# Two of eight batches turn their probabilities on TensorE instead of through DRAM, under new instruction orders

## The chip, the cores and the metric

The kernel runs on one core of a Trainium2 chip. Five engines of that core work from one program each, in order: PE (TensorE), DVE (VectorE), ACT (ScalarE), POOL (GpSimd) and SP (SyncE, which here only starts DMA transfers). They meet through semaphores. The metric is the time of one execution in microseconds (us). Three runs of the kernel before gave 583.65 us in the median (582.97 to 585.76). One more execution was taken by the hardware profiler, and all rows below come from it.

## The reference

The inputs q, k, v are (8 batches, 8 heads, 576 tokens, 64), in float32. Keys and values are first averaged over groups of 8 tokens, so that each of the 576 queries sees only 72 keys:

```python
k_p = k.reshape(B, H, 72, 8, D).mean(axis=3); v_p = ...the same of v
scores = scale * (q @ k_p.T); attn = softmax(scores); attn_out = attn @ v_p
x = attn_out, heads side by side            # (8, 576, 512)
h = relu(x @ w_in); u, v = halves of h      # w_in 512 x 1024
v_n = (v - mean(v)) / sqrt(var(v) + 1e-6)   # over the 512 features
v_s = w_spatial @ v_n + b_spatial           # 576 x 576, over the tokens
out = (u * v_s) @ w_out                     # w_out 512 x 512
```

w_in and w_out arrive in float64, the rest in float32. The spatial product mixes all tokens of a batch, so it starts only when the whole batch has been normalised.

## The kernel before

**Batches and stages.** Each batch goes through attention (capital letters) and then the gated block (small letters). K and V load and pool keys and values; KT turns the pooled keys; W splits the values; Q0 to Q3 load the queries, one per pair of heads (g); S0 to S3 are the scores and softmax of 512 tokens of such a head pair, U0 and U1 those of the last 64 tokens for two g at once; T0, T1 (512 tokens) and Y0, Y1 (the last 64) turn the probabilities of two g so that keys lie on partitions; A00 to A13 multiply probabilities with values (first digit: half of the tokens, second: g) and leave the result in xT. Then v0 to v4 (the v half of w_in, normalised), u00 to u13, s00 to s13 (the spatial product) and o0 to o4 (w_out). The weights are loaded and split in parts named wv, wu (w_in), wo (w_out), ws (w_spatial) and wb (bias). `warm` (wd) runs matmuls whose result nobody reads.

**Precision.** A product that has to be as good as float32 is made of three faster ones: each operand is split into a rounded high part and a low part (`split`: ACT writes the high part, DVE subtracts it from the source to get the low part), and TensorE adds high x high, low x high and high x low. This is why each stage of attention is followed by work on ACT and DVE.

**What sets the order.** Each stage is a Python generator that hands out a few instructions at each step. Three strings, FIRST, STEP and LAST, say which stage makes its next step; `-` and `+` shift the batch. FIRST runs the lead (loads, all weights, the first batch up to its first outputs), STEP runs once for each of six batches, and LAST ends the program. The instructions of each engine run in just that order. The marks `~^!%` behind a name choose another way of doing a stage: `^` pools on TensorE (`pool_pe`, L304) and loads queries by rows, to be turned on TensorE; any mark on V or K puts the pooling on POOL (`pool_sum`, L293 and L298) unless it is `^`. The mark that counts is the one at the first mention of the stage.

**The turning of probabilities before.** Softmax leaves a tile `e` with tokens on partitions and keys along the free axis; `pt_p` holds the last 8 keys of each head, copied on POOL. The matmul of A wants keys on partitions. In `att_pt` (T) DVE transposes blocks of 32x32 (tile X, L541; XR, L545), a DMA writes the tile to DRAM (xd, L549), and other DMAs read it back with the blocks in their places (pt_l, L556; pt_r, L560). `split_pt` then makes the high parts on ACT (pt_h L525, pt_rr L526) and the low parts on DVE (pt_l L528, pt_rr L531). `att_pt_l` (Y) does the same for the last 64 tokens (XL L569, xdl). The tiles pt_h, pt_l, pt_r and pt_rr have one buffer each, so the second pair of g (T1) can be written only after A has read the first pair (T0). A block layout goes with it: the pooled values lie on partitions in the order (key, block), and `half_of` says for each partition to which head of the pair it belongs.

**Shared buffers.** PSUM has three tiles `mm` (L304, weights, v, u, s, o), three tiles `tp` (transposes, U, A) and one `s` tile for the scores of S. The staging tiles `st` for keys, values, w_out and w_spatial share a ring of three; `g`, which DVE writes after each spatial product (L711), has three; ACT copies it rounded into gT (L717) and POOL writes the rest (gT, L720), which the o stage reads.

## Time and profile before

| what | value |
|---|---|
| median of 3 runs | 583.65 us (582.97 to 585.76) |
| the profiled execution's own time | 583.07 us |
| its span, first to last instruction | 581.3 us |
| so outside the span | 1.8 us |
| first matmul of v0 | 70.19 us |
| end of the last matmul | about 577.7 us |

How to read the rows that follow. The page opens with busy time per engine and then cuts the span into 40 slices of 14.5 us; each digit is a busy share in tenths, and PEclk is the clock that TensorE was granted. A row of grouped instructions reads: line, engine, operation, output tile <- input tiles, shapes, count, then busy us and mean ns of one, then the engine's idle time just before them and what ended it. A row of a timeline starts with the start time and the duration in us. A matmul's duration overlaps with the next one's, so the pace of matmuls is read from their starts. A row of waits gives the total, the number of times and the longest. A row of windows gives, for a stretch of time, its length, then busy time and count for PE, PEld, DVE, ACT and POOL, then the granted clock, the DMA share and GB/s.

### The profile page before, as it was taken

To read this page: it belongs to the slowest core of one execution; us is meant where nothing else is said; L and a number is where in the kernel's file an instruction comes from. 1 tells how busy PE (TensorE), PEld (TensorE's weight loads), DVE (VectorE), ACT (ScalarE), POOL (GpSimd) and SP (SyncE) were. 2 spreads that over 40 slices of the span, in tenths; PEclk is the share of its full clock that TensorE was granted. 3 is DMA by queue.
4 is the path that set the end of the run, shared out by engine and by line. 5 is a ranking of instruction groups with operands and counts; after the bars stand their busy time and mean duration, and the time that the engine had idled before them with its cause. 6 is when DMAs were issued, how large, how long until landed. Compare 5 with 4: busy or idle time off the path is not lost.

```text
span 581.3 us, 10183 instructions
## 1 busy us (share of the span) xinstructions
PE 554.3 (95%) x3428; PEld 499.6 (86%) x3428; DVE 395.5 (68%) x942; ACT 279.1 (48%) x832; POOL 247.2 (43%) x331
## 2 busy tenths in 40 slices
PE   5975899898999999999999999999999999999997
PEld 5865788796899889998899879988899889988995
DVE  2698789986875686868775877588776857433320
ACT  2545668834563355444553546435544475323321
POOL 3336576494655414433453325442643325303340
PEclk9796899999999999999999999999999999999999
DMA  8978624676753346234733356344622140200102
GB/s 228 262 212 230 144 77 117 171 211 173 215 122 89 98 134 132 54 95 164 188 67 95 127 147 124 84 104 150 124 55 74 73 115 24 75 36 1 37 2 90
DMA packets 134372, 68.61 MB, mean 118 GB/s; under 512 B 89136, under 2 KB 114736, under 8 KB 134320
## 3 DMA queue, kind: packets, MB, share of 16 engines
q1 hardware_dynamic: 134320, 67.96, 43.8%
q8 instruction: 27, 0.44, 0.3%
q14 instruction: 25, 0.20, 0.1%
HBM read 47.87 MB, written 20.05 MB: 117 GB/s over the span
## 4 chain that ended last, share of the span: by engine, by line
PE 82%; DVE 5%; DMA 5%; SPq 3%; POOL 2%; issue 1%; ACT 1%; DVEq 0%; ACTq 0%; POOLq 0%
PE mm L687 16%; PE mm L644 16%; PE mm L729 16%; PE mm L706 15%; PE s_ps L494 5%; PE mm L660 3%; DMA qt<-in_q 2%; PE tp L505 2%; PE tp L592 1%; PE mm L304 1%; PE tp L595 1%; PE mm L707 1%; PE mm L708 1%; PE tp L593 1%; PE tp L594 1%
## 5 line engine op out<-in xcount | busy, mean ns | idle before, releaser
L687 PE MATMUL mm<-xT,win_h 128*128 128x256 f32 (+1 forms) x512 | 103.6, 296 | 0.3 <-DVE wT_l L169 0.3
L720 POOL TENSOR_TENSOR gT<-g,gT 128x256 fp32r<-128x256 f32 x64 | 48.8, 765 | 87.7 <-ACT gT L717 87.7
L687 PEld LDWEIGHTS mm<-xT,win_h 128*128 128x128 f32 x512 | 82.8, 188 | 2.3 <-DVE wT_l L169 0.5
L729 PE MATMUL mm<-wout_h,gT 128*128 128x512 f32 x256 | 81.9, 400 | 0.6 <-POOL gT L720 0.6
L644 PE MATMUL mm<-win_h,xT 128*128 128x512 f32 x256 | 81.7, 400 | 0.0
L487 POOL TENSOR_TENSOR e<-e,rs 128x576 f32<-128x576 f32 (+1 forms) x48 | 49.1, 1022 | 71.4 <-DVE rs L485 56.1
L706 PE MATMUL mm<-wT_h,vn_h 128*128 128x256 f32 (+1 forms) x256 | 76.1, 297 | 2.4 <-ACT ru L690 2.4
L706 PE MATMUL mm<-wT_h,vn_l 128*128 128x256 f32 (+1 forms) x256 | 75.4, 295 | 0.0
L706 PE MATMUL mm<-wT_l,vn_h 128*128 128x256 f32 (+1 forms) x256 | 75.3, 294 | 0.0
L687 PE MATMUL mm<-xT,win_l 128*128 128x256 f32 (+1 forms) x256 | 75.3, 294 | 0.0
L711 DVE TENSOR_TENSOR g<-mm,ru 128x256 f32<-128x256 f32 (+1 forms) x64 | 28.6, 451 | 56.0 <-PE mm L708 48.9
L654 POOL TENSOR_TENSOR vn_l<-vv,vn_h 128x512 fp32r<-128x512 f32 x32 | 43.5, 1367 | 39.6 <-ACT vn_h L652 39.5
L717 ACT ACTIVATE gT<-g 128x256 fp32r<-128x256 f32 x64 | 26.3, 415 | 68.9 <-DVE g L711 68.9
L644 PEld LDWEIGHTS mm<-win_h,xT 128*128 128x128 f32 x256 | 46.8, 188 | 11.2 <-issue 1.0
L729 PEld LDWEIGHTS mm<-wout_h,gT 128*128 128x128 f32 x256 | 46.7, 188 | 11.3 <-issue 1.0
L631 POOL TENSOR_TENSOR rstd<-rstd,neg_half 128x1 f32<-128x1 f32 (+1 forms) x40 | 25.3, 635 | 72.2 <-DVE rstd L629 65.2
L706 PEld LDWEIGHTS mm<-wT_h,vn_h 128*128 128x128 f32 x256 | 48.2, 188 | 3.1 <-ACT ru L690 2.6
L644 PE MATMUL mm<-win_l,xT 128*128 128x512 f32 x128 | 50.6, 395 | 0.0
L729 PE MATMUL mm<-wout_l,gT 128*128 128x512 f32 x128 | 50.6, 395 | 0.0
L167 ACT ACTIVATE xT<-tp 128x320 fp32r<-128x320 f32 (+1 forms) x64 | 25.2, 410 | 51.8 <-PE tp L595 50.1
L706 PEld LDWEIGHTS mm<-wT_h,vn_l 128*128 128x128 f32 x256 | 48.2, 188 | 0.2
L687 PEld LDWEIGHTS mm<-xT,win_l 128*128 128x128 f32 x256 | 48.1, 188 | 0.0
(175 smaller groups left out, 1305.2 us busy)
## 6 DMA issues: line engine op xcount, KB each, us to landing
qt<-in_q SPq DMA_DIRECT2D x116, 72.0 KB, 3.1
st<-in_k SPq DMA_DIRECT2D x32, 256.0 KB, 3.1
st<-in_v SPq DMA_DIRECT2D x32, 256.0 KB, 4.7
xd<-X SPq DMA_DIRECT2D x32, 256.0 KB, 2.2
pt_l<-xd SPq DMA_DIRECT2D x32, 256.0 KB, 3.2
out<-ob SPq DMA_DIRECT2D x32, 256.0 KB, 2.1
stw<-in_moe_w_in SPq DMA_DIRECT2D x8, 512.0 KB, 5.9
pt_r<-xdr SPq DMA_DIRECT2D x32, 64.0 KB, 3.3
```

The source lines that it names most:

```text
L167: nc.scalar.activation(hi, src, AF.Copy)
L487: nc.gpsimd.tensor_tensor(em, em, rs.unsqueeze(2).broadcast_to([m, n, SP]), op=ALU.mult)
L494: nc.tensor.matmul(s_ps[:, c // 2, (c % 2) * 2 * SP:(c % 2 + 1) * 2 * SP], lhsT=t["q", g][:, c * P:(c + 1) * P], rhs=kp_bd[:, g, :], start ...
L631: nc.gpsimd.tensor_tensor(rstd[:m], rstd[:m], neg_half[:m], op=ALU.pow)
L644: nc.tensor.matmul(a, lhsT=xT[:, i, o + c * P:o + (c + 1) * P], rhs=w[:, i, DH:], start=(i == 0 and j == 0), stop=(i == NK - 1 and j == 2))
L654: nc.gpsimd.tensor_tensor(t["vn_l"][:, c, :], vv, f32(t["vn_h"][:, c, :]), op=ALU.subtract)
L687: nc.tensor.matmul(a, lhsT=w[:, i, d * P:(d + 1) * P], rhs=xT[:, i, o + ts.start:o + ts.stop], start=(i == 0 and j == 0), stop=(i == NK - ...
L706: nc.tensor.matmul(a, lhsT=x[:, c, ds], rhs=y[:, c, ts], start=(c == 0 and j == 0), stop=False)
L711: nc.vector.tensor_tensor(g, a, t["ru"][:, d, ts], op=ALU.mult)
L717: nc.scalar.activation(dst[:, d, 0, at:at + m], g[:, o:o + m], AF.Copy)
L720: nc.gpsimd.tensor_tensor(dst[:, d, 1, at:at + m], g[:, o:o + m], f32(dst[:, d, 0, at:at + m]), op=ALU.subtract)
L729: nc.tensor.matmul(a, lhsT=src[:, i, x, at:at + m], rhs=w[:, i, :], start=(i == 0 and j == 0), stop=(i == ND - 1 and j == 2))
```

## The change

1. **T and Y of batches 0 and 1** (`b < PE_B`, 2). PE turns the probabilities with the identity: for T, four transposes of 128x128 for each g and four of the last 8 keys (new lines L548, L552), into three `tp` tiles; for Y, two and one (L600, L601). ACT then writes pt_h and pt_rr straight from PSUM and DVE subtracts from PSUM. X, xd, and the reading back are gone for these two batches. Batches 2 to 7 keep the way through DRAM.
2. **The values of these two batches** are loaded in plain row order (one DMA for two g, where there were two), so that keys lie on partitions as the transposes leave them; `half` holds two versions of the head mask.
3. **warm** runs three more matmuls in float32r per call, but its calls fall from five (wd3, wd8, wd14, wd18, wd19, four matmuls of 128x128 in float32 each) to one (wd0).
4. **All three strings are new**, so each engine has another order throughout. The marks change with them: values of batches 2 to 7 are now pooled on POOL in all six batches (before in two), keys of batches 2 to 7 on DVE; one more query tile and one more split of a weight go through TensorE.

Three places in the new orders matter for what follows. The first is PE in the lead, around the scores S3 of batch 0 (L494 before, L501 now). Before:

```order
L304 MATMUL mm<-st,ident 128x128 x8
L505 MATMUL tp<-kp_bd,pt_q 64x144 x2
L266 MATMUL mm<-ident 128x128 x8
L494 MATMUL s_ps<-kp_bd,qT 128x144 x4
L304 MATMUL mm<-st,ident 128x128 x8
L304 MATMUL mm<-st_r,ident 64x64 x8
L592 MATMUL tp<-pt_h,vm_h 128x256
```

and now:

```order
L501 MATMUL s_ps<-kp_bd,qT 128x144 x4
L548 MATMUL tp<-ident,e 128x128 x8
L552 MATMUL tp<-ident,pt_p 32x128 x4
L304 MATMUL mm<-st,ident 128x128 x8
L512 MATMUL tp<-kp_bd,pt_q 64x144 x2
L304 MATMUL mm<-st,ident 128x128 x8
L304 MATMUL mm<-st_r,ident 64x64 x8
L636 MATMUL tp<-pt_h,vm_h 128x320
```

The scores S3 are followed at once by the transposes T0; the key pooling of batch 1 (L304) and U1 (L512) moved behind them, ahead of the first A (L636); the warm matmuls (L266) are gone from here.

The second is SP at the start of the program, the DMAs in the order in which they are started. Before:

```order
L327 DMA st<-in_k 128x1x512 x4
L183 DMA stw<-in_moe_w_in 128x1024
L314 DMA st_r<-in_k 64x1x512
L425 DMA qt<-in_q 128x4x64 x2
L426 DMA qt<-in_q 64x2x64
```

and now:

```order
L181 DMA stw<-in_moe_w_in 128x1024
L327 DMA st<-in_k 128x1x512 x2
L181 DMA stw<-in_moe_w_in 128x1024
L327 DMA st<-in_k 128x1x512 x2
L314 DMA st_r<-in_k 64x1x512
L432 DMA qt<-in_q 128x4x64 x2
L433 DMA qt<-in_q 64x2x64
```

A chunk of w_in (512 KB) now goes ahead of each half of batch 0's keys.

The third is POOL in the body, where batch n's spatial products are followed by the subtraction into gT while batch n+2's values arrive. Before (batch 3, the last whose values were pooled on POOL):

```order
L654 TENSOR_TENSOR vn_l<-vv,vn_h 128x512 x2
L487 TENSOR_TENSOR e<-e,rs 128x576
L498 COPY pt_p<-e 128x64
L720 TENSOR_TENSOR gT<-g,gT 128x256 x2
L720 TENSOR_TENSOR gt<-g,gt 128x64
L293 TENSOR_TENSOR st_r<-st_r 64x256
L293 TENSOR_TENSOR st_r<-st_r 64x128
L298 TENSOR_TENSOR vq<-st_r 64x64
L720 TENSOR_TENSOR gT<-g,gT 128x256 x4
```

and now, from the values of batch 4 on:

```order
L505 COPY pt_p<-e 128x64
L764 TENSOR_TENSOR gT<-g,gT 128x256 x2
L293 TENSOR_TENSOR st<-st 128x2x256
L293 TENSOR_TENSOR st<-st 128x2x128
L298 TENSOR_TENSOR vp<-st 128x128
```

The six instructions of a batch's main values (the last three rows, then the same three for the other two g) now stand between the second and the third gT, for batches 4 to 7; the values of batches 2 and 3 are spread over the lead.

The diff; in the strings only the first line of FIRST is shown, since the numbers in them tell a reader little:

```diff
--- before.py
+++ after.py
@@ -24,54 +24,49 @@
 FIRST = (
-    "-K^ -K wv0~% -K -K -Q1^ wv0 -K wv2~^ -Q1 -K wv2 -K -Q0^ wv0 wv0 -V^ wv1 -V -Q1 -KT~ -KT -Q0 K^ -KT wv0 "
...
+    "wv1~% wv1 -K^ wv1 wv0^% wv1 -K -K wv0 -Q0~^ wu3 wv0 -Q1^ -K -K -Q0 -K -K wd0 -KT~ -Q2^ -Q0 wo0^! -KT -KT "
...
 STEP = (
...
 LAST = (
...
@@ -140,13 +135,16 @@
     nc.gpsimd.memset(f32(vb[TL:]), 1.0)
 
 
-    half_of = const.tile([P, 2], F32, name="half_of")
+
+    half = const.tile([P, 2, 2], F32, name="half")
+    nc.vector.tensor_reduce(half[:, 0, 0:1], ident[:, :SP], axis=AX.X, op=ALU.add)
     by_block = ident.rearrange("p (s k) -> p k s", k=4)
     nb, ns = divmod(SP, 32)
-    nc.vector.tensor_reduce(half_of[:, 0:1], by_block[:, :nb, :], axis=AX.XY, op=ALU.add)
-    nc.vector.tensor_reduce(half_of[:, 1:2], by_block[:, nb, :ns], axis=AX.X, op=ALU.add)
-    nc.vector.tensor_tensor(half_of[:, 0:1], half_of[:, 0:1], half_of[:, 1:2], op=ALU.add)
-    nc.vector.tensor_scalar(half_of[:, 1:2], half_of[:, 0:1], -1.0, 1.0, op0=ALU.mult, op1=ALU.add)
+    nc.vector.tensor_reduce(half[:, 1, 0:1], by_block[:, :nb, :], axis=AX.XY, op=ALU.add)
+    nc.vector.tensor_reduce(half[:, 1, 1:2], by_block[:, nb, :ns], axis=AX.X, op=ALU.add)
+    nc.vector.tensor_tensor(half[:, 1, 0:1], half[:, 1, 0:1], half[:, 1, 1:2], op=ALU.add)
+    nc.vector.tensor_scalar(half[:, :, 1:2], half[:, :, 0:1], -1.0, 1.0, op0=ALU.mult, op1=ALU.add)
+    PE_B = 2
 
     mask = const.tile([2 * RR, 2], F32, name="mask")
     nc.vector.tensor_reduce(mask, ident[:2 * RR, :2 * RR].rearrange("p (s g) -> p g s", g=2), axis=AX.X, op=ALU.add)
@@ -264,6 +262,8 @@
         a = ps_tr() if i % 2 else ps_big()
         for _ in range(4):
             nc.tensor.matmul(a[:, :P], lhsT=ident, rhs=ident, start=True, stop=True)
+        for _ in range(3):
+            nc.tensor.matmul(a[:, :P], lhsT=ident_p, rhs=ident_p, start=True, stop=True)
         yield
 
     def load_w_sp(i):
@@ -367,12 +367,15 @@
         vp = pl.tile([P, NG, D], F32, name="vp", tag="vp")
         vq = pl.tile([2 * RR, 1, D], F32, name="vq", tag="vq")
         vr_s = pl.tile([RR, NG, D], F32, name="vr_s", tag="vr_s")
-        t["v"] = vp, vr_s
+        t["v"] = vp, vr_s, half[:, int(b >= PE_B), :]
         sts, g2 = [], [slice(2 * r, 2 * r + 2) for r in range(2)]
         for r in range(2):
             sts.append(ring("kv", 3, [P, 2, POOL * D], F32, "st"))
-            for i in range(2):
-                nc.sync.dma_start(out=sts[r][:, i, :], in_=rows[2 * r + i, :P].rearrange("(k s) f -> s k f", s=32))
+            if b < PE_B:
+                nc.sync.dma_start(out=sts[r], in_=rows[g2[r], :P].rearrange("g p f -> p g f"))
+            else:
+                for i in range(2):
+                    nc.sync.dma_start(out=sts[r][:, i, :], in_=rows[2 * r + i, :P].rearrange("(k s) f -> s k f", s=32))
             yield
         st = load_rest(*(rows[g, P:].rearrange("g s f -> s g f") for g in g2))
         yield
@@ -396,7 +399,7 @@
             nc.vector.tensor_tensor(vr_s[:, 2 * r:2 * r + 2, :], vq[rs].broadcast_to([RR, 2, D]),
                                     mask[rs].unsqueeze(2).broadcast_to([RR, 2, D]), op=ALU.mult)
 
-    def att_values_split(vp, vr_s):
+    def att_values_split(vp, vr_s, half_of):
         for e in range(2):
             nc.scalar.activation(vm_h[:, :, e, :], vp, AF.Copy, scale=half_of[:, e:e + 1])
         yield
@@ -415,6 +418,10 @@
     def by_tile(ap):
 
         return ap.rearrange("p (c q t) -> p q c t", c=NC, q=4)
+
+    def by_token(ap):
+
+        return ap.rearrange("p (q c t) -> p c q t", c=NC, q=4)
 
     def att_q(t, b, g, alt=""):
 
@@ -530,9 +537,31 @@
             yield
         nc.vector.tensor_tensor(rr[2 * RR:, cs], rw[:RR, cs], f32(rr[:RR, cs]), op=ALU.subtract)
 
-    def att_pt(t, j, alt=""):
+    def att_pt(t, b, j, alt=""):
 
         pm = [lambda g=g: t["p", g].rearrange("p (c e) s -> p c (e s)", e=2) for g in (2 * j, 2 * j + 1)]
+        if b < PE_B:
+            tps = []
+            for i in range(2):
+                tps.append(ps_tr())
+                for c in range(NC):
+                    nc.tensor.transpose(out=tps[i][:, c * P:(c + 1) * P], in_=pm[i]()[:, c, :P], identity=ident)
+                yield
+            tr = ps_tr()
+            for c in range(NC):
+                nc.tensor.transpose(out=tr[:RR, c * P:(c + 1) * P], in_=t["r", j][:, c, :, :], identity=ident)
+            yield
+            ph, pw, rw, rr = new_pt(t, j)
+            for i in range(2):
+                yield from split(by_token(ph[:, i, :NC * P]), by_token(pw.bitcast(F32R)[:, i, :NC * P]),
+                                 tps[i].rearrange("p (c q t) -> p c q t", c=NC, q=4))
+                yield
+            tv = tr[:RR].rearrange("p (c q t) -> p c q t", c=NC, q=4)
+            for i in range(2):
+                nc.scalar.activation(by_token(rr[i * RR:(i + 1) * RR, :NC * P]), tv, AF.Copy)
+            yield
+            nc.vector.tensor_tensor(by_token(rr[2 * RR:, :NC * P]), tv, by_token(f32(rr[:RR, :NC * P])), op=ALU.subtract)
+            return
 
 
         moved = []
@@ -562,9 +591,24 @@
             yield
         yield from split_pt(t, j, slice(0, NC * P), alt)
 
-    def att_pt_l(t, j, alt=""):
+    def att_pt_l(t, b, j, alt=""):
 
         em, pr = t["pl", j].rearrange("p (g e) s -> p g (e s)", g=2), t["r", j][:TL, NC, :, :]
+        if b < PE_B:
+            tp = ps_tr()
+            for i in range(2):
+                nc.tensor.transpose(out=tp[:, i * TL:(i + 1) * TL], in_=em[:, i, :P], identity=ident[:TL, :TL])
+            nc.tensor.transpose(out=tp[:RR, 2 * TL:3 * TL], in_=pr, identity=ident[:TL, :TL])
+            yield
+            ph, pw, rw, rr = new_pt(t, j)
+            yield from split(ph[:, :, NC * P:], pw.bitcast(F32R)[:, :, NC * P:],
+                             tp[:, :2 * TL].rearrange("p (g t) -> p g t", g=2))
+            yield
+            for i in range(2):
+                nc.scalar.activation(rr[i * RR:(i + 1) * RR, NC * P:], tp[:RR, 2 * TL:3 * TL], AF.Copy)
+            yield
+            nc.vector.tensor_tensor(rr[2 * RR:, NC * P:], tp[:RR, 2 * TL:3 * TL], f32(rr[:RR, NC * P:]), op=ALU.subtract)
+            return
         x = ring("XL", 1, [TL, 9, 32], F32, "XL")
         nc.vector.transpose(x[:, :8, :].rearrange("p (k g) s -> p g k s", g=2), em[:, :, :P].rearrange("p g (k s) -> p g k s", s=32))
         nc.vector.transpose(x[:, 8, :], pr.rearrange("p s g -> p (s g)"))
@@ -613,8 +657,8 @@
             st[f"S{g}"] = lambda g=g, **alt: att_softmax(t, g, **alt)
         for j in range(NG // 2):
             st[f"U{j}"] = lambda j=j, **alt: att_softmax_l(t, j, **alt)
-            st[f"T{j}"] = lambda j=j, **alt: att_pt(t, j, **alt)
-            st[f"Y{j}"] = lambda j=j, **alt: att_pt_l(t, j, **alt)
+            st[f"T{j}"] = lambda j=j, **alt: att_pt(t, b, j, **alt)
+            st[f"Y{j}"] = lambda j=j, **alt: att_pt_l(t, b, j, **alt)
         for half in range(2):
             for g in range(NG):
                 st[f"A{half}{g}"] = lambda half=half, g=g: att_av(t, half, g)
```

81 rows, old and new, of tables (FIRST, LAST, STEP) are left out of this document.

## The prediction

> **What bounds the kernel now.** I read the page first, then windows, then PE's waits. The page's head and its slices of 14.5 us:
>
> ```profile
> span 581.3 us, 10183 instructions
> PE 554.3 (95%) x3428; PEld 499.6 (86%) x3428; DVE 395.5 (68%) x942; ACT 279.1 (48%) x832; POOL 247.2 (43%) x331
> ...
> PE   5975899898999999999999999999999999999997
> ...
> PEclk9796899999999999999999999999999999999999
> ```
>
> PE is never below 9 after the tenth slice. Windows cut at the first v matmul and where the gaps end:
>
> ```profile
> 0.00:70.20 70.20, 51.70 (x344) 46.59 (x345) 48.79 (x109) 33.08 (x96) 30.28 (x37) 0.85 0.80 217
> 70.20:145.00 74.80, 69.88 (x431) 61.54 (x430) 64.12 (x148) 46.62 (x160) 48.11 (x58) 1.00 0.54 150
> 145.00:565.00 420.00, 420.00 (x2604) 381.57 (x2603) 282.62 (x687) 196.41 (x573) 166.99 (x234) 1.00 0.37 97
> ```
>
> From 145 to 565 us PE has work for all 420 us at clock 1.00. There nothing is to be had but PE work. In the lead PE is idle for 70.20 - 51.70 = 18.5 us, and its mean clock is 0.85; from 70.2 to 145 it is idle for 74.80 - 69.88 = 4.9 us. PE's waits:
>
> ```profile
> PE mm L304 <- DMA st<-in_k: 4.7, 1, 4.7
> PE tp L593 <- DVE vm_l L407: 3.9, 1, 3.9
> PE tp L592 <- ACT pt_h L525: 3.8, 1, 3.8
> PE mm L706 <- ACT ru L690: 2.4, 1, 2.4
> ```
>
> The first is for the first keys; the next two are the first A of batch 0, waiting for its operands; the last is in batch 1's lead. The chain of waits goes through the way by DRAM:
>
> ```profile
> 34.75 3.80 DMA xd<-X
> 38.62 3.77 DMA pt_l<-xd
> ...
> 42.47 1.06 ACT pt_h L525
> ```
>
> So the time is: when does v0 of batch 0 start, how much PE work follows, and how many gaps are in it.
>
> **Part 1: when v0 starts.** The lead before has these marks: POOL finishes the probabilities S1 and S3, DVE the last tile (pt_rr) of the first and of the second pair, PE begins v0.
>
> ```profile
> 31.91 1.15 POOL L487 TENSOR_TENSOR e<-e,rs 128x576 f32<-128x576 f32 x1 [3.48 <-DVE rs L485]
> 46.06 1.06 DVE L531 TENSOR_TENSOR pt_rr<-pt_r,pt_rr 32x512 fp32r<-32x512 f32 x1
> 49.05 1.15 POOL L487 TENSOR_TENSOR e<-e,rs 128x576 f32<-128x576 f32 x1 [1.86 <-DVE rs L485]
> 65.63 0.68 DVE L531 TENSOR_TENSOR pt_rr<-pt_r,pt_rr 32x512 fp32r<-32x512 f32 x1
> 70.19 0.62 PE L644 MATMUL mm<-win_h,xT 128*128 128x512 f32 x2
> ```
>
> That is 33.1, 47.1, 50.2, 66.3 and 70.2. The first pair takes 14.0 us from its probabilities to its tiles, the second 16.1. I walk the new order with durations from rows:
>
> ```profile
> L167 ACT ACTIVATE wT_h<-mm 128x512 fp32r<-128x512 f32 x4 | 2.4, 603 | 0.1
> L169 DVE TENSOR_TENSOR wT_l<-mm,wT_h 128x512 fp32r<-128x512 f32 x4 | 2.7, 674 | 0.1
> L531 DVE TENSOR_TENSOR pt_rr<-pt_r,pt_rr 32x512 fp32r<-32x512 f32 x16 | 12.5, 779 | 0.5
> L401 ACT ACTIVATE vm_h<-vp,half_of 128x256 fp32r<-128x256 f32 x16 | 7.2, 504 | 0.6 <-PE tp L594 0.6
> ...
> 17.61 2.29 PE L494 MATMUL s_ps<-kp_bd,qT 128*128 128x144 f32 x8
> 19.69 5.24 PE L304 MATMUL mm<-st,ident 128*128 128x128 f32 x32
> ...
> 44.13 0.30 ACT L480 ACTIVATE e<-s_ps,mx 128x72 f32<-128x72 f32 x1
> ...
> 46.50 0.64 ACT L221 ACTIVATE win_h<-x 128x512 fp32r<-128x512 f32 x1
> ...
> 88.25 0.60 PE L278 MATMUL mm<-ident,st 128*128 128x128 f32 x4
> 88.69 0.27 PE L280 MATMUL mm<-ident,st 128*64 128x128 f32 x1
> ```
>
> A transpose of 128x128 takes (88.69 - 88.25) / 4 = 0.11 us of PE at full clock, 0.14 or so when it is cold. ACT's copy of 512 columns out of PSUM is 0.60, DVE's subtraction from PSUM 0.67; I take the same for the new pt_h and pt_l, which read PSUM in permuted order (bounds: the same, and half as much again). Eight exponents of S with their sums take 46.50 - 44.13 = 2.4 us.
>
> - Keys: two weight chunks, 1 MB, now go ahead of the last of the keys, where one did, 0.5 MB; that is 2.4 us at the lead's 217 GB/s. The scores S0 then start at 19 to 20, not at 17.6. S0 to S3 share one score tile, and PE pools the values between S1 and S2 (5.2 us before, partly at half clock; some 4 now): S1 about 24, S2 30, S3 34. S1's probabilities are held up on POOL by 4.6 us of weight work and come at 33, as before. No gain up to here.
> - First pair: T0's 12 transposes wait for S3's scores only and end near 35.5. Then ACT sets the pace. From 32.2 (S2's scores at 30, then three passes of 0.7 us on DVE and ACT) it has pooled values 0.6, pt_rr of Y0 0.5, vm_h and vr 4 x 0.5, a weight 0.6, pt_h 2 x 0.6, eight exponents 2.4, pt_rr 2 x 0.6: 8.5 us, so 40.7. DVE's last pt_rr ends 0.8 later, **41.5**. Before: 47.1.
> - Those eight exponents are S3's. Its probabilities come at 41, not at 50.2, because the weight conversions that stood ahead of S3 on DVE (four instructions of 0.65 us or so for a chunk) moved behind it.
> - Second pair: T1's transposes follow the A of the first pair, near 47. DVE sets the pace: from 41.5 a weight 2.3, four xT and a sum 3.0, two weights 3.8, pt_l 2 x 0.67, pt_rr 0.8, waits 0.3: 11.5 us, so **53.0**. Before: 66.3.
> - From there A02, KT of batch 1, w_spatial, a weight split, A03, S0 of batch 1, A12 and A13 are 6 us of PE, so **59** for v0.
>
> 59 is a walk without lateness. The trace shows what lateness is like: the weight conversion's mean is 651 ns (row below) though most take 0.43. I add 2.5 us and take **61.5**. If the cold clock stays as it was it is more:
>
> ```profile
> L199 DVE TENSOR_SCALAR x<-x 128x512 uint32<-128x512 uint32 x12 | 7.8, 651 | 7.3 <-ACT x L194 7.2
> ...
> 35.00:37.50 2.50, 2.50 (x23) 2.50 (x23) 2.43 (x5) 0.95 (x2) 2.09 (x2) 1.00 1.03 333
> 42.50:45.00 2.50, 0.58 (x1) 0.29 (x1) 2.37 (x9) 2.43 (x8) 0.00 (x0) 0.66 0.99 315
> 65.00:67.50 2.50, 2.37 (x12) 2.07 (x12) 2.44 (x6) 0.51 (x2) 0.00 (x0) 0.56 0.53 86
> ```
>
> The clock was 1.00 while PE was fed at 35, and half after the 3.8 us in which the first A waited. In the new order the pooling of batch 1's keys and U1 fill that gap, so I expect no drop there; if half clock comes all the same for the last 10 us of PE work, it costs 5 more. Bounds for v0: 59.0 and 66.5. Against 70.2 the forecast is **-8.7** (-11.2 to -3.7).
>
> **Part 2: PE work behind v0.** Batch 1 turns after v0: 24 transposes for T, 6 smaller ones for Y, 30 x 0.11 = **+3.3** at most, with PE as the bound and nothing to hide them. In return one warm call is gone:
>
> ```profile
> 115.18 1.06 PE L266 MATMUL tp<-ident 128*128 128x128 f32 x8
> 115.99 0.40 PE L592 MATMUL tp<-pt_h,vm_h 128*128 128x320 f32 x1
> ```
>
> 115.99 - 115.18 = **-0.8**. The weight splits behind v0 are as many as before. Batch 0's 30 transposes and the other warm calls lie ahead of v0 and are in part 1.
>
> **Part 3: gaps behind v0**, 4.9 us. The 2.4 of L706 come while ACT waits for pt_l of batch 1 with the ru copies queued behind it; that wait is gone with the DMA. But the lead is now shorter by 9 us and the rest of the weights must come that much sooner. I keep 3.0 of the 4.9: **-1.9** (0 to -3.9).
>
> **Sum.** -8.7 + 3.3 - 0.8 - 1.9 = -8.1. The profiled execution took 583.07 (its span and 1.8 us around it), which gives 575.0; it lies 0.6 under the median of 583.65, so for the median **575.5**. All cheap: 583.65 - 11.2 + 2.5 - 3.9 = 571.0. All dear: 583.65 - 3.7 + 2.5 = 582.5.
>
> **What costs nothing, and its cover.** The DMA traffic that is gone frees no time of itself: behind 70 us the DMA engines are busy 0.54 and less. DVE loses the pooling of values in most batches; it had slack. STEP's new order costs nothing if PE stays fed: the cover there is DVE's 137 us of slack in 420.
>
> **The rivals.**
>
> *A: v0 hardly moves, since the way by DRAM was not all that bound the lead.* For it: DVE is busy 48.8 of 70.2 us and the weights still have to go through it, POOL gets more weight work; the walk ends on DVE for pair two. Against it: pair one takes 14.0 us, of which DVE works a third. It gives the dear end, 582.5.
>
> *B: slower, through POOL in the body.* The six instructions of a batch's values now stand between the second and third gT. Their rows and a wait that this once made:
>
> ```profile
> L293 POOL TENSOR_TENSOR st<-st 128x512 f32<-128x512 f32 x4 | 5.2, 1290 | 0.0
> L293 POOL TENSOR_TENSOR st<-st 128x256 f32<-128x256 f32 x4 | 2.9, 736 | 0.3
> L298 POOL TENSOR_TENSOR vp<-st 128x128 f32<-128x128 f32 x4 | 1.8, 461 | 0.3
> ...
> PE mm L729 <- POOL gT L720: 0.6, 1, 0.6
> ...
> 177.61 1.43 PE mm L706 x12
> ```
>
> 2 x (1.29 + 0.74 + 0.46) = 5.0 us. Behind them on POOL is gT; DVE waits for gT to free one of three g tiles, and the spatial products on PE wait for DVE. Twelve matmuls of 256 columns take 1.43, so a product (14) takes 1.7, or 2.1 with 320 columns. Counted from the first product's start, with S and A of the next batch between, the sixth needs its g at 13.4 us, and the third gT is through at 10.7: 2.7 us to spare. If the values land later than that on SP's queue, each of batches 4 to 7's loads costs PE the excess. From 2.0 us of stall in each of four batches the gain of 8.1 is eaten; with 3 us it is 575.5 + 12 = 587.5. Against it: the first of these loads is started a whole stage ahead.
>
> *C: the clock.* If transposes leave PE cold, the 16 us of PE work from 41 us to v0 take twice as long; v0 comes at 74, +3.8, and the sum is 583.65 + 3.8 + 2.5 - 1.9 = 588. For it: five calls of warm matmuls became one. Against it: transposes are under a tenth of that work, and the row at 35 us shows the clock at 1.00 under ordinary matmuls. The Trainium skill ("TensorE: Matmul & The Clock Gate", Part 4: PE-mode transpose) speaks for C: it says that a transpose does not count as PE activity for the clock gate the way a matmul does. No row here has transposes alone for long enough to say; by that rule the sum would be C's.
>
> **How the numbers follow.** The forecast 0.70, A 0.16, B 0.10, C 0.04. About 0.5%, 2.9 us, is what a measurement of this kernel can tell from no change. The forecast's own range, 571 to 580, is faster; A is within; B and C slower. So faster 0.70, same 0.16, slower 0.14. The range reaches from 571.0 to 583.0, past A, and leaves out B, C and a walk that beats 59.
>
> **What would show it.** v0 (now L688) starting at 59 to 64 us; no wait of L636 (A) over 2 us; PEclk without a half-clock slice at 43 to 53; PE with no idle time from 145 to the end; PE busy in the span 2 to 3 us more behind v0. The forecast is wrong if v0 starts after 67, if PE waits in the body again and again for DVE g or POOL gT, or if the wait of the first A now names ACT or DVE for 4 us and more.

## The result, and the profile after

| | time, us | against the kernel before |
|---|---|---|
| before | 583.50 (4 runs) | |
| after | 569.6 (569.42 to 569.70) | 0.9754 [0.9722, 0.9786] |
| after, measured a second time | 569.37 (4 runs) | 0.9752 [0.9721, 0.9784] |

The change makes the kernel 13.9 us faster. The forecast was 575.5, with a range of 571.0 to 583.0: the sign is right, the gain was taken too small, and the time lies 1.4 us below the range. The profiled execution of the first measurement was disturbed (910 us at a clock of 0.56; the ratio and the range leave it out, and the other three have a median of 569.5), so the rows here are from the second measurement of the same kernel, whose profiled execution took 568.92 us.

The page's head and slices (14.2 us each now) of the kernel after:

```profile
span 567.1 us, 10236 instructions
PE 551.8 (97%) x3468; PEld 496.2 (87%) x3468; DVE 384.5 (68%) x894; ACT 288.7 (51%) x903; POOL 274.3 (48%) x367
...
PE   5989999999999999999999999999999999999996
...
PEclk9999999999999999999999999999999999999999
```

PE is at 9 from the fourth slice on, but for the last one, and no slice has a lower clock. Windows of the kernel after, cut at v0 (58.0 us):

```profile
0.00:58.00 58.00, 47.19 (x362) 40.99 (x363) 45.46 (x99) 34.56 (x96) 33.24 (x41) 1.00 0.81 216
58.00:145.00 87.00, 87.00 (x526) 76.17 (x525) 72.33 (x178) 55.13 (x199) 61.87 (x77) 1.00 0.53 133
145.00:560.00 415.00, 415.00 (x2575) 377.33 (x2574) 266.72 (x619) 198.03 (x609) 179.18 (x251) 1.00 0.34 92
560.00:567.10 7.10, 2.56 (x12) 1.74 (x10) 0.00 (x0) 1.02 (x2) 0.00 (x0) 1.00 0.27 74
```

and the same cut of the kernel before behind its v0 (70.19 us):

```profile
70.19:145.00 74.81, 69.89 (x431) 61.55 (x430) 64.13 (x148) 46.63 (x160) 48.12 (x58) 1.00 0.54 150
145.00:574.00 429.00, 429.00 (x2642) 388.83 (x2641) 282.62 (x687) 198.18 (x576) 168.79 (x237) 1.00 0.37 96
574.00:581.30 7.30, 3.68 (x16) 2.63 (x14) 0.00 (x0) 1.17 (x2) 0.00 (x0) 1.00 0.35 105
```

From v0 on PE now has no idle time until its last matmul. The spans differ by 14.2 us, and the windows split that without a rest:

| term | before | after | change | forecast |
|---|---|---|---|---|
| start of v0 | 70.19 | 57.98 | -12.2 | -8.7 |
| PE busy behind v0 | 502.6 | 504.6 | +2.0 | +2.5 |
| PE idle between v0 and its last matmul | 4.9 | 0 | -4.9 | -1.9 |
| last matmul's end to the span's end | 3.6 | 4.5 | +0.9 | 0 |
| sum | | | -14.2 | -8.1 |

All PE waits of half a microsecond and more that are left lie in the lead:

```profile
PE mm L304 <- DMA st<-in_k: 6.8, 1, 6.8
PE tp L552 <- DVE pt_rr L610: 1.5, 1, 1.5
PE s_ps L501 <- DVE qT L454: 0.8, 1, 0.8
PE tp L600 <- POOL e L494: 0.6, 1, 0.6
PE tp L636 <- DVE pt_rr L610: 0.5, 1, 0.5
PE s_ps L501 <- DVE kp_bd L359: 0.5, 1, 0.5
```

The waits of 3.8 and 3.9 us of the first A and the 2.4 us for ru are gone. The marks of the lead, from the timeline (scores S0 and S3 on PE; probabilities S1 and S3 on POOL; the last 512-token tile of each pair and that of Y1 on DVE; v0):

```profile
17.57 1.22 PE L501 MATMUL s_ps<-kp_bd,qT 128*128 128x144 f32 x8 [0.52 <-DVE kp_bd L359]
30.34 1.25 PE L501 MATMUL s_ps<-kp_bd,qT 128*128 128x144 f32 x8 [0.80 <-DVE qT L454]
...
30.24 1.15 POOL L494 TENSOR_TENSOR e<-e,rs 128x576 f32<-128x576 f32 x1
38.24 1.15 POOL L494 TENSOR_TENSOR e<-e,rs 128x576 f32<-128x576 f32 x1 [1.78 <-DVE rs L492]
...
39.01 0.68 DVE L563 TENSOR_TENSOR pt_rr<-tp,pt_rr 32x512 fp32r<-32x512 f32 x1
50.17 0.68 DVE L563 TENSOR_TENSOR pt_rr<-tp,pt_rr 32x512 fp32r<-32x512 f32 x1
52.29 2.31 DVE L197 TENSOR_SCALAR x<-x 128x512 uint32<-128x512 uint32 x1
54.63 0.22 DVE L610 TENSOR_TENSOR pt_rr<-tp,pt_rr 32x64 fp32r<-32x64 f32 x1
57.98 0.40 PE L688 MATMUL mm<-win_h,xT 128*128 128x512 f32 x1
```

| mark, end in us (S0: start) | before | forecast | after |
|---|---|---|---|
| S0's scores start | 17.6 | 19 to 20 | 17.6 |
| S1's probabilities | 33.1 | 33 | 31.4 |
| S3's scores | 36.9 | 34 | 31.6 |
| first pair's last 512-token tile | 47.1 | 41.5 | 39.7 |
| S3's probabilities | 50.2 | 41 | 39.4 |
| second pair's last 512-token tile | 66.3 | 53.0 | 50.9 |
| v0 starts | 70.2 | 59, and 2.5 for lateness: 61.5 | 58.0 |

### The profile page after: what moved, and what is told of

The parts are those of the page before. It is cut to its first block, busy times and chain, and to the rows that moved or that the text cites. A ratio compares the mean times of both kernels' runs of the same rounds, so it can differ in the third digit from the quotient of the medians.

```text
span 908.3 us, 10236 instructions
## 1 busy us (share of the span) xinstructions
PE 896.1 (99%) x3468; PEld 691.1 (76%) x3468; DVE 365.6 (40%) x894; ACT 289.8 (32%) x903; POOL 270.5 (30%) x367
## 4 chain that ended last, share of the span: by engine, by line
PE 99%; DMA 1%; SPq 0%; DVE 0%; issue 0%; ACT 0%; ACTq 0%; DVEq 0%
PE mm L731 18%; PE mm L773 18%; PE mm L750 18%; PE mm L688 16%; PE s_ps L501 6%; PE mm L304 4%; PE mm L704 3%; PE tp L512 2%; PE mm L751 2%; PE mm L752 2%; PE tp L636 2%; PE tp L637 2%; PE tp L639 2%; PE tp L638 2%; PE mm L223 1%; PE tp L548 1%
## 5 line engine op out<-in xcount | busy, mean ns | idle before, releaser
L731 PE MATMUL mm<-xT,win_h 128*128 128x320 f32 (+1 forms) x512 | 158.4, 410 | 0.0
L688 PE MATMUL mm<-win_h,xT 128*128 128x512 f32 x256 | 124.2, 582 | 0.0
L773 PE MATMUL mm<-wout_h,gT 128*128 128x512 f32 x256 | 123.6, 579 | 0.0
L731 PEld LDWEIGHTS mm<-xT,win_h 128*128 128x128 f32 x512 | 112.7, 239 | 10.4 <-issue 1.6
L750 PE MATMUL mm<-wT_l,vn_h 128*128 128x256 f32 (+1 forms) x256 | 105.0, 410 | 0.0
L731 PE MATMUL mm<-xT,win_l 128*128 128x256 f32 (+1 forms) x256 | 104.7, 409 | 0.0
L750 PE MATMUL mm<-wT_h,vn_h 128*128 128x256 f32 (+1 forms) x256 | 104.1, 407 | 0.0
L750 PE MATMUL mm<-wT_h,vn_l 128*128 128x256 f32 (+1 forms) x256 | 104.0, 406 | 0.0
L494 POOL TENSOR_TENSOR e<-e,rs 128x576 f32<-128x576 f32 (+1 forms) x48 | 48.7, 1014 | 168.4 <-DVE rs L492 157.0
L688 PEld LDWEIGHTS mm<-win_h,xT 128*128 128x128 f32 x256 | 55.5, 220 | 39.9 <-issue 22.6
L773 PEld LDWEIGHTS mm<-wout_h,gT 128*128 128x128 f32 x256 | 55.4, 219 | 38.6 <-issue 22.9
L773 PE MATMUL mm<-wout_l,gT 128*128 128x512 f32 x128 | 73.7, 576 | 0.0
L750 PEld LDWEIGHTS mm<-wT_l,vn_h 128*128 128x128 f32 x256 | 62.9, 246 | 3.4
```

Of the source, the lines that this page charges most:

```text
L494: nc.gpsimd.tensor_tensor(em, em, rs.unsqueeze(2).broadcast_to([m, n, SP]), op=ALU.mult)
L688: nc.tensor.matmul(a, lhsT=xT[:, i, o + c * P:o + (c + 1) * P], rhs=w[:, i, DH:], start=(i == 0 and j == 0), stop=(i == NK - 1 and j == 2))
L731: nc.tensor.matmul(a, lhsT=w[:, i, d * P:(d + 1) * P], rhs=xT[:, i, o + ts.start:o + ts.stop], start=(i == 0 and j == 0), stop=(i == NK - ...
L750: nc.tensor.matmul(a, lhsT=x[:, c, ds], rhs=y[:, c, ts], start=(c == 0 and j == 0), stop=False)
L773: nc.tensor.matmul(a, lhsT=src[:, i, x, at:at + m], rhs=w[:, i, :], start=(i == 0 and j == 0), stop=(i == ND - 1 and j == 2))
```

## The experiments

Four questions were open: is it the way on TensorE or the new orders that brings the gain; is the extra gain PE's clock; do batch 1's transposes cost or pay; and what sets the lead and the end now. No kernel here leaves out any of the computation.

**The kernel after once more**, unchanged, for the profile above:

> The changed kernel once more, for a profile of an undisturbed execution (569.6 us, 13.9 less than before; 8.1 were forecast). Theory 'lead': the missing 5.8 us are in the lead, because the walk carried the half clock of the kernel before along; then v0 starts at 55 to 57 us instead of 61.5, the granted clock is 1.00 in every slice of the lead, and what lies behind v0 is as forecast (about 3.3 us of transposes more, 0.8 of warm matmuls less, 3.0 of 4.9 us of gaps left). Theory 'behind': v0 starts at 59 to 62 and the stretch behind v0 is 5 us shorter than forecast: no gap of PE over 0.3 us from v0 to 145 us, or fewer or denser matmuls in the body.

Measured: 569.37 us. The answer is a mixture. v0 is 3.5 us ahead of the forecast, as 'lead' said though not quite so far, with the clock at 1.00 throughout; and all gaps behind v0 are gone, as 'behind' said.

### Way and orders, each alone

**New orders, all batches through DRAM.**

```diff
-    PE_B = 2
+    PE_B = 0
```

> The new orders with all batches turned through DRAM (PE_B = 0): T and Y of batches 0 and 1 and the loading of their values as before. Theory 'way': the transposes on TensorE bring the gain; each pair of the first batch then waits 7.6 us for DRAM again, less the 2 to 3 us that a turn on PE takes, so v0 comes 8 to 12 us later than in the changed kernel, behind v0 2.5 us of transposes are gone but the waits for the tiles of batch 1 are back: 577 to 582 us. Theory 'orders': the new orders bring most of it: within 3 us of 569.6.

Measured: 599.73 us, 1.0265 [1.0236, 1.0294] of the kernel before, 30 us over the kernel after. PE's longest wait in it:

```profile
PE tp L636 <- ACT pt_h L532: 12.2, 3, 6.8
```

v0 starts at 78.6, 20.6 us later than in the kernel after, where the theory 'way' had 8 to 12; it had the direction only. The new orders without the new way lose some 15.5 us against the kernel before, and PE stands idle for pt_h, 12.2 us in three places. The longest of them is ahead of the first A: DVE's last block transpose of the first pair ends at 37.6, pt_h is written at 47.0, and PE has run out of other work at 40.2.

**The way alone for batch 0, under the old orders.** The strings and the warm calls are those of the kernel before; in FIRST the steps of batch 0's T0 (shown) and T1 are put together:

```diff
-    PE_B = 2
+    PE_B = 1
...
-"... -S1 -T0 -V ... -T0 -S2 ... -T0 -S2 wv3 -T0 wd8 ... -T0 ... -T0 ... -T0 ... -T0 ..."
+"... -S1 -T0 -V ... -S2 ... -T0 -T0 -T0 -T0 -T0 -T0 -T0 -T0 -S2 wv3 wd8 ..."
```

> The kernel before with one part of the change alone: batch 0 (not batch 1) turned on TensorE, its values in plain rows; all three orders and the warm calls as before, only the eight or nine steps of its T0 and T1 stand together where the old steps of the first pair's third place and the second pair's seventh were. Theory 'way': the first A no longer waits 3.8 and 3.9 us for pt_h and vm_l, and the second pair's tiles come some 7 us sooner: v0 at 60 to 64, 574 to 578 us. Theory 'orders': the old order of the weights on ACT and DVE and of S3 keeps the second pair where it was: v0 at 66 to 70, 580 to 584 us.

Measured: 594.40 us, 1.0179 [1.0147, 1.0211]. Both theories missed: it is slower than before. The 512-token tiles came as promised, but not what else an A product needs (DVE's timeline, then the first wait of the list of waits):

```profile
39.25 0.68 DVE L563 TENSOR_TENSOR pt_rr<-tp,pt_rr 32x512 fp32r<-32x512 f32 x1 [2.00 <-ACT pt_rr L561]
49.60 1.25 DVE L410 SCALAR_TENSOR_TENSOR vm_l<-vp,half,vm_h 128x256 fp32r<-128x256 f32 x2
```
```profile
PE tp L637 <- DVE vm_l L410: 6.6, 1, 6.6
```

The first pair's tiles are ready at 39.9, where it was 47.1. But in the old DVE order the low part of the values (vm_l) stands behind two weight conversions and the maximum of S3, and comes at 50.9. And T0's transposes now stand ahead of S3 on PE, and S3's scores start at 39.95 instead of 35.76. v0 starts at 77.5.

**The same with vm_l moved forward**, so that the first A need not wait for it:

```diff
-"... -T0 -S2 wv3 ... K -W ws0 -W -A00 ..."
+"... -T0 -W -W -S2 wv3 ... K ws0 -A00 ..."
```

> The kernel before with batch 0 turned on TensorE (594.4 us), and one move more: the values' low parts (vm_l, vr; two steps of W) stand on DVE right behind T0's instructions, no longer behind two weight conversions and the softmax of S3. If the order of DVE is what took the gain of the transposes, the first A runs through from 44 us on instead of waiting 6.6 us for vm_l, and v0 comes 5 to 7 us sooner: 587 to 590 us. If the second pair is bound elsewhere (S3 and the conversions, which stand where they stood): within 2 us of 594.

Measured: 595.83 us, 1.0209 [1.0164, 1.0254]: no gain. vm_l is ready at 41.1, and PE waits at the next place instead:

```profile
PE tp L636 <- DVE xT L169: 5.2, 3, 2.2
PE tp L636 <- DVE pt_rr L610: 4.7, 1, 4.7
```

So neither part was worth anything by itself as it was tried: the orders alone cost some 15.5 us, the way for batch 0 alone some 10.4, together they gain 14. Two things were not tried under the old orders: both batches on TensorE, and T0's transposes behind S3 on PE, where the new orders have them. What the way alone could gain at best is therefore open.

### Batch 1's part

```diff
-    PE_B = 2
+    PE_B = 1
```

> The changed kernel with batch 1 turned through DRAM again (PE_B = 1); batch 0 stays on TensorE. It prices the part of the change that lies behind v0. As forecast, batch 1's 30 transposes cost PE 3.3 us with nothing to hide them, so if DRAM were quick enough for these orders the time falls to 566 to 567. If the waits for batch 1's tiles come back (the kernel with all batches through DRAM had 8.4 us of PE waits behind v0), it rises to 572 to 578, and the transposes have paid for themselves behind v0 too.

Measured: 579.94 us, 0.9926 [0.9902, 0.9951], 10.6 over the kernel after. v0 starts at 58.1, as with both batches on TensorE, so all of this lies behind it. The waits behind v0 add up to 7.3 us:

```profile
PE mm L731 <- ACT ru L734: 2.2, 1, 2.2
PE tp L638 <- DVE pt_l L535: 1.2, 2, 0.8
PE mm L731 <- DVE wT_l L167: 1.2, 1, 1.2
PE tp L639 <- DVE pt_rr L538: 1.2, 1, 1.2
PE tp L636 <- ACT pt_h L532: 1.1, 1, 1.1
PE mm L750 <- DVE wT_l L167: 0.4, 1, 0.4
```

and PE runs at half clock twice, for some 3.4 us after the longest of them and for some 6.7 us from 120 us on, among the waits for pt_h, pt_l and pt_rr (windows of this run):

```profile
85.90:89.80 3.90, 3.87 (x16) 3.87 (x17) 3.79 (x10) 2.32 (x5) 0.33 (x1) 0.56 0.07 17
118.00:130.00 12.00, 9.36 (x35) 7.77 (x35) 7.87 (x14) 6.59 (x28) 9.19 (x13) 0.72 0.44 114
```

In the first of these windows PE does 16 matmuls where the kernel after does 27. The 3.3 us of transposes that the forecast booked as a loss keep more than 10 us of waits and slow work away.

### The clock

**The kernel before, kept warm.** The first form:

```diff
-    def att_av(t, half, g):
+    def att_av(t, half, g, warmers=0):
...
+        for _ in range(warmers):
+            nc.tensor.matmul(o[:, :P], lhsT=ident, rhs=ident, start=True, stop=True)
         nc.tensor.matmul(o, lhsT=h2, rhs=mh[:, ts], start=True, stop=False)
...
-                st[f"A{half}{g}"] = lambda half=half, g=g: att_av(t, half, g)
+                st[f"A{half}{g}"] = lambda half=half, g=g: att_av(t, half, g, 70 if (b, half, g) == (0, 0, 0) else 0)
...
-"... -Q1 -KT~ -KT ... -V -U0 wv2 ..."
+"... -Q1 wd1 wd5 -KT~ -KT ... -V wd7 -U0 wv2 ..."
```

> The kernel before with PE kept busy in three of its gaps by matmuls that nobody reads: 8 of 128x128 ahead of the turning of the first keys, 4 ahead of U0, 70 ahead of the first A; nothing else is changed. Theory 'clock': the half-clock stretches at 16 to 23 and 43 to 53 us vanish, the first eight A products run at full speed (2.7 us less) and S0 and S1 come some 2 us sooner, so v0 comes 3 to 5 us sooner: 579 to 581 us; so much of the 13.9 us is the clock alone. Rival 'not the clock': v0 waits for the second pair's tiles on DVE and ACT (66.3) whatever PE's clock: 583 to 584 us.

Measured: 591.11 us, 1.0128 [1.0088, 1.0168]. The 70 needless matmuls took 15.9 us, not 8; the second matmul of the first A, the one that had waited for vm_l, ran at 55.4 instead of 48.1, and v0 came later by nearly as much, at 77.2. That says only that v0 hangs on the first A. The second form has 35 of them, and wd1 alone of the three calls:

> The first kernel of this kind put 15.9 us of needless matmuls ahead of the first A, where 8 were meant, since a float32 matmul of 128x128 took 0.23 us and not 0.11. Now 35 of them (8.0 us, from 39.7 to 47.7, the wait for pt_h and vm_l) and 4 ahead of the turning of the first keys. Theory 'clock': no half clock at 43 to 53, the A products of the first pair end near 50.5 instead of 53.0, and v0 comes 2 to 3 us sooner: 580.5 to 582. Rival 'tiles': v0 waits for the second pair's way through DRAM, DVE and ACT, which does not depend on PE's clock: within 1 us of the kernel before.

Measured: 584.07 us, 1.0015 [0.9991, 1.0039], no difference. Its windows:

```profile
16.00:40.00 24.00, 21.88 (x178) 19.14 (x176) 19.68 (x46) 12.06 (x37) 9.40 (x12) 1.00 0.85 239
40.00:57.00 17.00, 13.66 (x110) 12.71 (x110) 15.14 (x31) 9.37 (x33) 7.95 (x8) 1.00 0.81 222
57.00:62.00 5.00, 4.08 (x14) 2.86 (x15) 1.92 (x7) 1.20 (x3) 4.82 (x4) 0.66 0.92 271
```

The clock was 1.00 from 16 to 57 us (0.86 and 0.70 in the same two windows before), and still v0 starts at 70.6 instead of 70.2. PE only waits longer at the next place (3.1 us for wT_l at 57.9 instead of 2.1). The clock falls behind that wait, where it was 1.00 before, but PE then waits another 2.0 us for win_l, so this drop is covered. The second pair's last tile is ready at 66.5 instead of 66.3. In the lead of the kernel before, then, a higher clock from 16 to 57 us gained nothing; the rest of the chain to the second pair's tiles did not get shorter.

**The kernel after without its warm call, and with transposes in its place.**

```diff
-"... -K -K wd0 -KT~ -Q2^ ..."
+"... -K -K -KT~ -Q2^ ..."
```

> The changed kernel without its one warm call (seven matmuls of 128x128 that nobody reads, 1.4 us of PE between the pooling of the keys and the turning of the keys). Theory 'clock': the gap of PE from 14.4 to 15.7 us opens, the granted clock falls to half near 16.5 us for some 6 us, as it did before, and S0, the value pooling and S1 take 2 to 3 us longer: v0 at 60 to 61, 571.5 to 573 us. Rival 'not the clock': PE is only idle there, the clock stays 1.00: 569 to 569.8 us.

Measured: 569.87 us, 0.9755 [0.9729, 0.9781]. The theory 'clock' is right on the drop and wrong on its size: it lasts 3.4 us instead of 6, and v0 starts at 59.3, not at 60 to 61:

```profile
17.00:18.00 1.00, 0.66 (x3) 0.69 (x4) 0.93 (x4) 0.35 (x2) 0.00 (x0) 0.72 0.64 184
18.00:19.00 1.00, 1.00 (x6) 1.00 (x5) 0.80 (x2) 0.00 (x0) 0.00 (x0) 0.50 0.99 379
```

From S0's start to v0 it takes 42.0 us here and 40.4 in the kernel after, so in the new orders a drop in the lead does cost time, 1.6 us in this execution. The median differs by 0.5 us only, which these intervals do not separate.

```diff
-        for _ in range(4): nc.tensor.matmul(a[:, :P], lhsT=ident, rhs=ident, ...)
-        for _ in range(3): nc.tensor.matmul(a[:, :P], lhsT=ident_p, rhs=ident_p, ...)
+        for _ in range(12): nc.tensor.transpose(out=a[:, :P], in_=ident, identity=ident)
```

> The changed kernel with the warm call's seven matmuls replaced by twelve transposes of 128x128, which keep PE as long (1.3 us). With the matmuls the granted clock stayed 1.00; without any it fell to half from 17.3 to 20.5 us and v0 came 1.3 us later. If transposes count for the clock as matmuls do: clock 1.00, v0 at 58.0, 569.4. If they do not: half clock near 17 us, v0 at 59 to 59.5, 569.9 to 570.5.

Measured: 569.51 us, 0.9754 [0.9732, 0.9777], and no drop at that place:

```profile
18.00:19.00 1.00, 0.58 (x5) 0.62 (x6) 0.93 (x4) 0.42 (x2) 0.00 (x0) 1.00 0.94 352
```

S3 starts 12.77 us after S0, exactly as in the kernel after (14.34 without any warm call). Yet v0 starts at 59.4, which the expectation had given to the other theory: S0 came 0.8 us later, at 18.4, and a drop came later in this execution, from about 53.5 to 57 us. The rows of PE in the 25 us ahead of it are the same as in the kernel after and in the run without a warm call, and neither of these two has a drop there. So the same work of PE can leave the clock up in one execution and not in another, and one execution of each kernel does not settle whether transposes count.

### The body

**Values of batches 3 to 7 pooled on DVE again** (rival B):

```diff
-"... +U0 ++V~ +Q3 ..."
+"... +U0 ++V +Q3 ..."
...
-"+V~ U0 -o3 -A12 ..."
+"+V U0 -o3 -A12 ..."
```

> The changed kernel with one mark taken away: the values of batches 2 to 7 are pooled on DVE, not on POOL. If the pooling on POOL between the gT subtractions costs PE nothing (forecast), this is the same or, since DVE gets 6 x 5 us of work, up to 3 us slower: 569.6 to 573. If POOL did stall PE (rival B), it is faster by what it stalled: under 568.

Measured: 572.08 us, 0.9781 [0.9743, 0.9818]. The mark of batch 2 stands earlier in FIRST and was not changed, so its values stay on POOL; the edit covers five batches, not the six of the expectation. There is no stall of POOL to take away, and on DVE a small one appears: three waits of the spatial product for g, 1.2 us together. Most of the rest of its profiled execution's length is not the edit's: v0 started at 60.5, 2.5 us later than in the kernel after, though nothing ahead of it is changed. That is the next point.

### What sets the lead and the end now

**Keys first**, as before the change:

```diff
-"wv1~% wv1 -K^ wv1 wv0^% ..."
+"-K^ wv1~% wv1 wv1 wv0^% ..."
```

> The changed kernel with the first half of the keys ahead of the first chunk of w_in on SP's queue, as before the change; that chunk follows at once. PE waits 6.8 us for the first keys (4.7 before the change). If the chain from the keys through S2 sets the lead, v0 comes up to 2.1 us sooner: 567.5 us. If the second half of the keys, which still stands behind both chunks, or DVE's and ACT's weight work sets it: 569 to 570 us, no change.

Measured: 571.94 us, 0.9790 [0.9765, 0.9816]: neither theory, it is slower by 2.6. PE starts 2.1 us sooner, then waits for the second half of the keys, and then works on it at a granted clock of about a half (the last row is a window):

```profile
4.72 3.76 PE L304 MATMUL mm<-st,ident 128*128 128x128 f32 x16 [4.72 <-DMA st<-in_k]
11.46 3.20 PE L304 MATMUL mm<-st,ident 128*128 128x128 f32 x16 [2.98 <-DMA st<-in_k]
...
12.00:15.50 3.50, 3.50 (x19) 3.17 (x17) 2.32 (x3) 0.00 (x0) 2.33 (x2) 0.51 0.72 163
```

S0 starts at 19.9 and v0 at 60.35, 40.42 us later. In the kernel after it is 40.41, in the run with the values on DVE 40.42, in the run with batch 1 through DRAM 40.43. So the lead behind S0 is rigid while the clock stays up, and what moves S0 moves all of it.

Two things move S0. One is the arrival of the keys' second half: PE goes on with it at 11.5 here, at 11.0 in the run with Y0's step moved (below). The other is larger, PE's pace on it: the 16 matmuls took 3.2 us here and 2.0 there. The two runs further down that move steps of Y show the pace alone:

```profile
11.01 2.02 PE L304 MATMUL mm<-st,ident 128*128 128x128 f32 x16 [1.09 <-DMA st<-in_k]
10.82 3.75 PE L303 MATMUL mm<-st,ident 128*128 128x128 f32 x16 [0.67 <-DMA st<-in_k]
```

The first row is of the run with Y0's step moved, where S0 starts at 17.9; the second is of the run with Y1's step moved as well, which has the same program up to there (its L303 is the same line): the data came no later, and S0 started at 19.9. In the new kernels S0 starts at 17.3 to 18.4 where this part ran at full pace, or nearly, and at 19.9 to 20.0 in the three profiled executions where it did not. What decides the pace is not shown; the gaps ahead of the second half were 2.98, 1.14 and 0.67 us in the three slow cases and 0 to 1.09 in the others.

**Two results of DVE moved ahead of slow instructions.**

```diff
-"... -S1 -Y0 -T0 -S2 -V wo0 -W -Y0 -T0 wu3 ..."
+"... -S1 -Y0 -Y0 -T0 -S2 -V wo0 -W -T0 wu3 ..."
```

> The changed kernel with one DVE instruction moved: the last step of Y0 (pt_rr, L610, 0.2 us) ahead of the masking of the values' rest (1.6 us) and of a weight instruction (0.4). In the changed kernel PE's third group of transposes of T0 waits 1.5 us for it, since it frees their tile. Theory 'DVE's order sets the lead now': that wait goes and v0 comes 1 to 1.5 us sooner, 568 to 568.4. Rival 'PE's wait there is slack': ACT's eight exponents and the copies of the pair's tiles (33.2 to 38.6) end as before, v0 at 58 within 0.5, 569.0 to 569.8.

Measured: 569.82 us, 0.9758 [0.9726, 0.9790]; S0 to v0 takes 40.5. The rival holds. The wait of 1.5 us is not gone, it moved one group of matmuls on:

```profile
PE tp L512 <- DVE pt_l L167: 1.5, 1, 1.5
```

Then Y1's last step as well:

```diff
-"... -Y1 -Y1 ws0 Q1 wv2 wu2 wu0 wb -Y1 +K~ ..."
+"... -Y1 -Y1 -Y1 ws0 Q1 wv2 wu2 wu0 wb +K~ ..."
```

> As the run before, and the last step of Y1 as well, ahead of a weight instruction on DVE that took 2.31 us in the changed kernel (0.43 in the median), so that A03 of the first half no longer stands behind it. Theory 'DVE's order': v0 another 1 to 1.7 us sooner: 566.5 to 567.5. Rival: the late instruction then delays S0 of batch 1 or the next xT instead, since DVE is busy nine tenths of that stretch: 568.5 to 569.5.

Measured: 570.22 us, 0.9777 [0.9740, 0.9814]. Again nothing is won; the time is even 0.7 above the rival's range. The profiled execution tells little, since its v0 at 61.7 has S0 late, as said, and half clock from 56.5 to 59.9 us.

**The last two products exchanged.**

```diff
-"... o3 o3 o3 o2 o4 o2 o4 o2 o4"
+"... o3 o3 o3 o4 o2 o4 o2 o4 o2"
```

> The changed kernel with the last two products of the last batch exchanged: o4 (two output transfers of 64 rows, one after the other on SP's queue) ahead of o2 (one of 128 rows). From the last matmul's end to the span's end there were 4.5 us, 3.6 before the change, where o2 stood last. Expected: 3.6 again, the time 0.9 less, 568.5 us. Rival: the transfer's own latency sets it whichever is last: no change.

Measured: 568.42 us, 0.9740 [0.9716, 0.9764]. In the kernel after, the last copy is followed by two transfers on SP; here by one (a row's second number is SP's time to issue them):

```profile
563.26 1.12 SPq L783 DMA_DIRECT2D out<-ob  x2
```
```profile
563.75 0.34 SPq L780 DMA_DIRECT2D out<-ob  x1
```

From PE's end (562.67 + 0.39) to the end of the span (566.7) it is 3.6 us, where the kernel after has 4.5. The gain of 0.95 us was the one expected; the intervals of the two ratios overlap, so it rests on this end of the trace. All three edits together:

> The two moves on DVE and the exchange of the last two products together. If they add up, 0.95 less than the kernel with the two moves alone: 565.5 to 566.6 by the theory 'DVE's order', 567.6 to 568.5 by its rival.

Measured: 568.85 us, 0.9763 [0.9722, 0.9804]: 0.35 above the rival's range and far from the other. The exchange's gain is there; of the two moves the profile has 0.2 us at most (S0 to v0 takes 40.2 us instead of 40.4). The exchange without the moves, 568.42, is the best version seen, 15 us faster than the kernel before.

## Why the prediction was right and wrong

**What bounds the kernel**: right. The gain is the sum of an earlier v0, the gaps behind it and the PE work behind it; from 145 us on nothing changed but the length of PE's work.

**Part 1, -8.7, was -12.2.** The mechanism stands: the tiles of both pairs came sooner and S3's probabilities 11 us sooner. The 3.5 that the forecast lacked can be read from the table of marks in three pieces.
- The step that failed is the first bullet, "S0 then start at 19 to 20" and "No gain up to here". The keys did come later, by 2.1 us, but S0 started at 17.6 all the same: before, PE waited 0.95, 0.80 and 0.64 us for a query, the pooled keys and pt_q between the pooling and S0, and of these 2.4 us only one wait of 0.5 is left (rows of the kernel before):

```profile
PE tp L440 <- DMA qt<-in_q: 1.0, 1, 1.0
PE tp L350 <- ACT kp L343: 0.8, 1, 0.8
PE tp L505 <- ACT pt_q L448: 0.6, 1, 0.6
```

  The walk added the delay to S0 and did not look at the waits behind it that would absorb it. S1's probabilities came at 31.4 instead of 33: **1.6**.
- From S1's probabilities to the first pair's tile the walk gave 8.5 and it took 8.3; from there to the second pair's 11.5 and 11.2. ACT's and DVE's sums of rows held: **0.5** together.
- The 2.5 of lateness were 1.1, if the walk's last 6 us are taken as right: **1.4** too much. One late instruction is seen, the weight conversion at 52.29, which took 2.31 us where 0.43 is usual; PE waited 0.5 us for Y1's tile behind it. (POOL ran a cast of 0.60 and a subtraction of 1.27 us in that time; that they held the conversion up is not shown.) Moving what stood behind such instructions did not help. DVE is busy 45 of the lead's 58 us; in the first of the two runs the wait of 1.5 us only moved on by one group of matmuls.

That the clock would stay up was right, but the clock alone would have gained nothing: the kernel before, kept at full clock from 16 to 57 us, started v0 no sooner. In the new orders it is needed, as the 1.6 us lost without the warm call show. The walk's 0.14 us for a cold transpose was too low, since the row of four at 50.88 in the kernel before gives 0.21 at half clock, but no term used it. The bound of 59.0, taken as a walk without any lateness, was no bound, because its opening was too long by more than the lateness that came.

**Part 2, +2.5, was +2.0** in PE work. As an account of batch 1's transposes it was too narrow: without them the new orders wait 7.3 us behind v0 and run some 10 us at half clock, and the time is 10.6 us longer.

**Part 3, -1.9, was -4.9.** The failed step is "the lead is now shorter by 9 us and the rest of the weights must come that much sooner. I keep 3.0". PE waited for no weight behind v0, and for nothing else. With that term at its full 4.9 alone the sum would have been -11.1, and 572.5 the forecast. The range's cheap end let only 3.9 of the 4.9 go.

**The end, 0, was +0.9**: not looked at. The order puts o4 with its two transfers last; exchanging it gave the 0.95 back.

**The rivals.** A (v0 hardly moves) and B (POOL stalls PE in the body) did not come: no wait for gT or g is left, and with the values of five batches back on DVE the time is 2.7 us longer, some of it by the edit. C (a cold clock) did not come either. The Trainium skill ("TensorE: Matmul & The Clock Gate", Part 4: PE-mode transpose) has it that a transpose does not count as PE activity for the clock in the way a matmul does. The profiled execution with twelve transposes in place of the warm matmuls speaks against it, since the clock stayed at 1.00 there, and S3 came 12.77 us after S0 with the one as with the other. It is one execution with 1.4 us of transposes among other matmuls, and does not refute the rule.

A rival that was not named came nearest to a trap: that the change is worth its gain only as a whole. Each half of it, as tried here, was measured as a loss of some 10 or 15 us.

## What to carry to other kernels

A shorter way for one operand and the order of the engines around it are one change: measured alone, either can lose about as much as both together win, so a failed half proves nothing against the whole. Gaps of the bounding engine that hang on the way which is removed should be booked as gone unless a row names what would take their place. Where a lead is rigid from its first large product on, look for what delays that product, and at the program's other end for what follows the last one.

## What the runs showed that was not expected

- **The first PE work after the start runs at half pace while the clock column says 1.00.** In the run with the values on DVE, 16 matmul records of the key pooling took 3.75 us at 6.6, and 16 more after a gap of 1.14 us took 3.67. In the kernel after, 32 of the same shape (the pooling of the values) took 3.73 us at 22.6. The first two of these rows:

```profile
6.62 3.75 PE L304 MATMUL mm<-st,ident 128*128 128x128 f32 x16 [6.62 <-DMA st<-in_k]
11.51 3.67 PE L304 MATMUL mm<-st,ident 128*128 128x128 f32 x16 [1.14 <-DMA st<-in_k]
```

- **The clock can halve with only short gaps ahead.** In the run without the warm call it fell at 17.4 us and stayed down for 3.4, with no gap of PE over 0.6 us in the 4 us ahead. The kernel after had a gap of 1.5 us at 32.5 and no drop. The Trainium skill ("TensorE: Matmul & The Clock Gate", Why this matters for your kernels) puts the danger at gaps of more than about 3 us; this run shows a drop well below that.
- **A lead of 40 us repeats to 0.03 us** (40.40 to 40.43 in one execution each of five kernels that have the same orders from S0 to v0 and kept the clock up), while the start of S0 moved by up to 2.5 us, most of it with PE's pace on the second half of the keys.
